# Fixed turns of the PSUM banks, and VectorE's side work set half a gap apart, in an attention and MLP kernel

## The chip, the cores and the metric

The kernel runs on one core of a Trainium2 chip. A core has five engines with a queue of instructions each: TensorE (PE in the profile, its weight loads PEld), VectorE (DVE), ScalarE (ACT), GpSimd (POOL) and SyncE (SP), which here only starts transfers. Each engine takes its own instructions strictly in the order in which the program lists them, and waits where an instruction needs the result of another engine. TensorE writes its results to PSUM, which has eight banks of 512 float32 numbers in each of 128 partitions; VectorE and ScalarE read them from there.

The metric is the device time of one execution in microseconds. Before the change the median of three executions is 1475.52 us (1472.6 to 1476.87); the profiled execution has a span of 1474.3 us.

## The reference

All data are float32. q, k and v have the shape (8, 12, 448, 64): 8 batches, 12 heads, 448 positions, 64 numbers a head. In short:

```
q_n = q / sqrt(mean(q*q) + 1e-6) * g_q          # the same for k with g_k
scores = q_n @ k_n.T / sqrt(64)                 # 448 x 448 for each batch and head
attn = exp(scores - max) / (sum + 1e-9)
x = (attn @ v), heads side by side              # 3584 rows of 12*64 = 768
h = x @ w_in                                    # 3584 x 2048
g = h - tanh(h)
out = g @ w_out                                 # 3584 x 768
```

The weights are given as float64, of which the kernel reads the two words and rounds them itself.

## The kernel before

The work is written as one long program in which the author's order is kept on every engine; the framework only adds the waits. It adds them from the tiles: an instruction that reads or writes a tile waits for the earlier ones on other engines that it must not overtake.

**Attention steps.** A step is one batch and one pair of heads, 48 in all. For a step `load` fetches q, k and v; `squares` (ScalarE) and `norm` (L365: two sums and two small operations on VectorE, two powers on GpSimd) give the factors of the norm; `norm_q` (L376) multiplies q by its factors on VectorE. `turn` (L385) transposes k and q on TensorE into two banks, and ScalarE copies them out as kT (L392) and qT (L398). `scores` (L404) multiplies them for one of four groups of keys into two banks, one for each head, and ScalarE takes the exponentials (L422). `add` (L430) adds up the exponentials of the key groups on VectorE: two additions over three full groups (L438, L439) and two over the last, half group (L442). `totals` (L470) sums them over the keys with a product with ones, and VectorE takes the reciprocal (L490). `last_values` (L444) and `values` (L457) multiply by v into two banks, and `divide` (L492) multiplies the result by the reciprocals in four operations (L498) and writes x, transposed.

**The MLP.** `mlp` is a generator of matmuls. Both layers use a form of blocked product with seven products instead of eight for each set of output blocks, in the order 1, 5, 6, 2, 3, 7, 4 (`products`, L532). In the hidden layer a product is 6 matmuls of 128x128 by 224 columns, in the output layer 8 (each shows as two records in the profile). When a product is done, its bank is read at once by one or two operations (`use`): L607 to L623 and the tanh and subtraction L589 and L590 for the hidden layer, L670 to L684 for the output layer. Products 2, 3 and 7 go on in the banks of 1, 5 and 6. A hidden layer has four sets for each batch, the output layer three. The first batch's output layer is an ordinary product instead (`project_first`, L718 and L724), because its weights are still being prepared.

**How the two are laid together.** `first_slot` works through the first steps without the MLP. From step 6 on, `slot` (L792) writes one step with four stretches of the MLP between its parts: `run(gap)` draws matmuls from the generator until as much time of TensorE is used up as the gap asks for. In a slot from step 12 on, a gap is 14 matmuls (28 records). In the order of the code: scores of key groups 0 and 1 of the next step, a gap, the transposes of the step after that, a gap, scores of the last keys, values of the last keys, sums, the other values, divisions, scores of key group 2, `add`, `norm`, a gap, `norm_q`, a gap. What stays of the MLP after the last step runs alone at the end.

**The banks.** `mm_bank` (L152) takes a bank for the MLP from a pool of three, `sc_bank` (L401) one for attention from a pool of five. In the first slots attention uses both. Each call makes a new tile of one bank, and the pool decides which of its banks that is, from what has been given back.

Of the kernel before, what the change touches and what calls it, by code (L numbers as in the profile page):

```python
# [9 lines left out]
F32 = mybir.dt.float32  # L10
# [5 lines left out]
PSUM = bass.MemoryType.PSUM  # L16
# [76 lines left out]
def bounded_path(tc, ctx, q, k, v, moe_w_in, moe_w_out, out, g_col, ident, ones, half_ones, neg_half):  # L93
# [20 lines left out]
    P = 128  # L114
# [15 lines left out]
    KF, KR = S // P, S % P  # L130
# [3 lines left out]
    def pool(name, **kw):  # L134
        return ctx.enter_context(tc.tile_pool(name=name, **kw))
# [10 lines left out]
    gp = pool("gp", bufs=1)  # L146
    wp_stack = ctx.enter_context(ExitStack())
    wp = wp_stack.enter_context(tc.tile_pool(name="wp", bufs=1))
    ps_s = pool("ps_s", bufs=5, space=PSUM)
    ps_m = pool("ps_m", bufs=3, space=PSUM)  # L150

    def mm_bank():  # L152
        return ps_m.tile([P, 512], F32, name="mm")

    loaded = {}

    def load(s, names):
        b, hp = steps[s]
        for name in names:
            src = {"q": q, "k": k, "v": v}[name]  # L160
            bufs = 3 if name == "v" else 2
            pair = src[b, 2 * hp : 2 * hp + 2]
            if name == "q":
                t = nat.tile([CP, 2, NCH, D], F32, name="q_nat", bufs=bufs)
                nc.sync.dma_start(
                    out=t.rearrange("p h c d -> p h (c d)"), in_=pair.rearrange("h (p c) d -> p h (c d)", c=NCH)
                )
            else:
                full, rest = pair[:, :K0].rearrange("h (p c) d -> h p c d", c=KF), pair[:, K0:]
                if name == "v":  # L170
                    t = nat.tile([P, 2, NCH, D], F32, name="v_nat", bufs=bufs)
                    last = t[:, :, KF]
                    nc.sync.dma_start(
                        out=t[:, :, :KF].rearrange("p h c d -> p h (c d)"), in_=full.rearrange("h p c d -> p h (c d)")
                    )
                else:
                    t = nat.tile([P, NCH, 2, D], F32, name="k_nat", bufs=bufs)
                    last = t[:, KF]
                    for h in range(2):
                        nc.sync.dma_start(out=t[:, :KF, h], in_=full[h])  # L180
                for r in range(2):
                    nc.sync.dma_start(out=last[r * KR : (r + 1) * KR], in_=rest.rearrange("h p d -> p h d"))  # L182
            loaded[name, s] = t
# [103 lines left out]
    def combine(count):  # L287
        for j, p, dst, x, y, op in combos[:count]:
            nc.vector.tensor_tensor(out=dst, in0=x, in1=y, op=op)
            if p == 7:  # L290
                kept[0] = j + 1
        del combos[:count]
# [63 lines left out]
    normed, turned, probs, sums, whole, xT, tt = {}, {}, {}, {}, {}, {}, {}  # L356
# [8 lines left out]
    def norm(s):  # L365

        sq, n = normed[s]
        rr = small.tile([P, 2, 2 * NCH], F32, name="rr", bufs=3)
        for i, rows in ((1, CP), (0, P)):
            r = rr[:rows, i]  # L370
            nc.vector.reduce_sum(r, sq[i], axis=AX.X)
            nc.vector.tensor_scalar(out=r, in0=r, scalar1=1.0 / D, scalar2=1e-6, op0=ALU.mult, op1=ALU.add)  # L372
            nc.gpsimd.tensor_tensor(out=r, in0=r, in1=neg_half[:rows], op=ALU.pow)  # L373
        normed[s] = rr, n

    def norm_q(s):  # L376
        rr, n = normed[s]
        t = loaded.pop(("q", s))
        nc.vector.tensor_tensor(
            out=n.rearrange("p c h d -> p h c d"), in0=t,  # L380
            in1=rr[:CP, 1].rearrange("p (h c) -> p h c", h=2)[:, :, :, None].to_broadcast([CP, 2, NCH, D]),
            op=ALU.mult,
        )

    def turn(s, tk, tq):  # L385

        rr, n = normed.pop(s)
        kn = loaded.pop(("k", s))
        for c in range(NCH):
            nc.tensor.transpose(tk[:, c * P : (c + 1) * P], kn[:, c].rearrange("p h d -> p (h d)"), ident)  # L390
        kT = qkp.tile([P, S], F32, name="kT")
        nc.scalar.mul(kT, tk[:, :S], g_col)  # L392
        for c in range(NCH):
            nc.tensor.transpose(  # L394
                tq[:, c * CP : (c + 1) * CP], n[:, c].rearrange("p h d -> p (h d)"), ident[:CP, :CP]
            )
        qT = qkp.tile([P, S], F32, name="qT")
        nc.scalar.copy(out=qT, in_=tq[:, :S])  # L398
        turned[s] = rr, kT, qT

    def sc_bank():  # L401
        return ps_s.tile([P, 512], F32, name="sc")

    def scores(s, c):  # L404

        rr, kT, qT = turned[s]
        halves, keys, n = (1, P, S) if c < KF else (2, KR, HS)
        name, bufs = ("p", 2) if c < 2 else ("p_full", 1) if c < KF else ("p_last", 2)
        if c == 1:
            p = probs[s, 1] = probs[s, 0]  # L410
        else:
            p = probs[s, c] = pp.tile([P, 2, 2 if c < 2 else 1, n], F32, name=name, bufs=bufs)
        tiles = [sc_bank() for _ in range(2)]
        for i in range(halves):
            for h in range(2):
                r = slice(h * D, (h + 1) * D)
                nc.tensor.matmul(  # L417
                    tiles[h][i * keys : (i + 1) * keys, :n], lhsT=kT[r, c * P : c * P + keys],
                    rhs=qT[r, i * n : (i + 1) * n], start=True, stop=True,
                )  # L420
        for h in range(2):
            nc.scalar.activation(  # L422
                p[:, h, c if c < 2 else 0, :], tiles[h][:, :n], AF.Exp, scale=rr[:, 0, 2 * c + h : 2 * c + h + 1]
            )

    def full(s):

        return probs[s, 0][:, :, 0], probs[s, 1][:, :, 1], probs[s, 2][:, :, 0]

    def add(s):  # L430

        if s <= NP + NP // 2:
            sums[s] = []
            return
        t = sp.tile([P, 2, S], F32, name="sum")
        sums[s] = [t]
        p, last = full(s), probs[s, KF][:, :, 0]
        nc.vector.tensor_tensor(out=t, in0=p[0], in1=p[1], op=ALU.add)  # L438
        nc.vector.tensor_tensor(out=t, in0=t, in1=p[2], op=ALU.add)  # L439
        for n in range(2):  # L440
            part = t[n * KR : (n + 1) * KR, :, n * HS : (n + 1) * HS]
            nc.vector.tensor_tensor(out=part, in0=part, in1=last[n * KR : (n + 1) * KR], op=ALU.add)  # L442

# [297 lines left out]
    def run(ns):  # L741

        spent[1] += ns
        while spent[0] + 1.0 < spent[1]:
            took = next(stream, None)
            if took is None:
                return
            spent[0] += took
# [10 lines left out]
    def has(s):  # L759
        return 0 <= s < NS  # L760

    def first_slot(s):

        if has(s + 1):
            scores(s + 1, 0)
            scores(s + 1, 1)
        if has(s + 2):
            turn(s + 2, mm_bank(), sc_bank())
        if s > -3:
            load(s + 4, "qk")  # L770
        squares(s + 3)
        norm(s + 3)
        if has(s):
            totals(s, mm_bank())
        if has(s + 2):
            load(s + 2, "v")
        if has(s + 1):
            scores(s + 1, KF)
        if has(s):
            av = [mm_bank() for _ in range(2)]  # L780
            last_values(s, av)
            values(s, av)
        if has(s + 1):
            scores(s + 1, 2)
            add(s + 1)
        norm_q(s + 3)
        if has(s):
            divide(s, av)
        weight(EARLY * (s + 3) // (NP + 2))
        combine(2)  # L790

    def slot(s):  # L792
        gap = gap_ns(s)
        if s < 2 * NP:
            totals(s, sc_bank())
        if has(s + 1):
            scores(s + 1, 0)
            scores(s + 1, 1)
        if has(s + 2):
            load(s + 2, "v")  # L800
        run(gap)
        if has(s + 2):
            turn(s + 2, sc_bank(), sc_bank())
        if has(s + 3):
            squares(s + 3)
        if has(s + 4):
            load(s + 4, "qk")
        run(gap)
        if has(s + 1):
            scores(s + 1, KF)  # L810
        dn = sc_bank() if s >= 2 * NP else None
        av = [sc_bank() for _ in range(2)]
        last_values(s, av)
        if s >= 2 * NP:
            totals(s, dn)
        divide(s, values(s, av))
        if has(s + 1):
            scores(s + 1, 2)
            add(s + 1)
        if has(s + 3):  # L820
            norm(s + 3)
        run(gap)
        if has(s + 3):
            norm_q(s + 3)
        run(gap)

    load(0, "qk")
    load(1, "qk")
# [335 lines left out]
```

## Time and profile before

| what | before |
|---|---|
| time, median of three | 1475.52 us |
| span of the profiled execution | 1474.3 us |
| TensorE busy | 1434.7 us (97%) |
| VectorE busy | 809.9 us (55%) |
| ScalarE busy | 455.3 us (31%) |
| GpSimd busy | 508.5 us (34%) |
| TensorE matmuls of the MLP (L553), of the chain that ended last | 63.7% |

The page's busy table tells how long each engine worked. Its ends of matmuls are modelled, so whether TensorE really had no pause is read from its waits: a wait is idle time of an engine just before an instruction, put down to the instruction on another engine that ended it. In a list in order of time, each line is a start in us, a length in us, the engine, the line of the kernel, the operation, what is written and read, how many instructions were merged into the line (x), and in brackets the idle time ahead of it with its cause. Bank tiles have the names `sc` and `mm`.

The program has four stretches: loading and the first steps (to about 109 us), the first batch of the MLP beside attention and the preparation of the weights (to about 297 us), 36 equal slots, and the last batch of the MLP alone.

### The profile page before, as it was taken

What the parts mean: (1) busy time and instruction counts of PE and PEld (TensorE: products, weight loads), DVE (VectorE), ACT (ScalarE), POOL (GpSimd) and SP (SyncE); (2) the same over time, 40 slices, a digit from 0 to 9 for tenths busy, and PEclk for the clock granted to TensorE, in tenths of its full rate; (3) what the DMA queues carried; (4) which work ended last, traced back from release to release, by engine and by line L of the source; (5) the groups of instructions that cost most, each with busy time, mean ns of one, the idle gap of its engine ahead of it and who ended that gap; (6) DMA issues with size and microseconds to landing.
All of it is one profiled execution on the core that took longest, in us unless ns stands there. A gap on an engine that the chain in (4) does not pass through costs nothing.

```text
span 1474.3 us, 26066 instructions
## 1 busy us (share of the span) xinstructions
PE 1434.7 (97%) x10272; PEld 1186.9 (81%) x10272; DVE 809.9 (55%) x1245; ACT 455.3 (31%) x850; POOL 508.5 (34%) x378
## 2 busy tenths in 40 slices
PE   6989899999999999999999999999999999999997
PEld 2558664488888888888888888888888888899997
DVE  3997888755554565347535654555555366433322
ACT  5754553133212332223322233213322233200100
POOL 4655656323331334213422233232333133312310
PEclk9999999999999999999999999999999999999999
DMA  8767787864556544654555555546555654455563
GB/s 177 171 190 201 244 252 204 230 186 148 167 145 175 174 143 144 187 166 149 185 141 169 151 163 162 163 138 182 154 167 142 167 183 135 148 166 157 187 191 97
DMA packets 268055, 250.74 MB, mean 170 GB/s; under 512 B 164884, under 2 KB 210196, under 8 KB 267924
## 3 DMA queue, kind: packets, MB, share of 16 engines
q1 hardware_dynamic: 267600, 248.97, 58.0%
q8 instruction: 84, 1.38, 0.4%
q14 instruction: 47, 0.39, 0.1%
q10 hardware_dynamic: 324, 0.00, 0.0%
HBM read 215.48 MB, written 33.42 MB: 169 GB/s over the span
## 4 chain that ended last, share of the span: by engine, by line
PE 89%; DVE 5%; DMA 2%; SPq 2%; ACT 1%; issue 1%; POOL 0%; ACTq 0%; DVEq 0%; POOLq 0%
PE mm L553 64%; PE sc L417 9%; PE sc L464 6%; PE mm L718 5%; PE sc L485 2%; PE sc L452 1%; PE sc L390 1%; PE sc L394 1%; SPq L182 1%; DVE rs L490 1%; SPq L230 1%; DVE xT L498 1%; PE mm L464 0%; DVE w_out L78 0%; DMA gT<-in_moe_w_in_dram 0%
## 5 line engine op out<-in xcount | busy, mean ns | idle before, releaser
L553 PE MATMUL mm<-xT,w_f 128*128 128x224 f32 x1392 | 280.8, 355 | 4.6 <-DVE s L619 4.6
L553 PEld LDWEIGHTS mm<-xT,w_f 128*128 128x128 f32 x1392 | 259.3, 190 | 25.5 <-issue 9.8
L553 PEld LDWEIGHTS mm<-gT,w_f 128*128 128x128 f32 x1344 | 251.4, 190 | 22.5 <-issue 11.4
L553 PE MATMUL mm<-gT,w_f 128*128 128x224 f32 x1344 | 267.7, 355 | 0.0
L373 POOL TENSOR_TENSOR rr<-rr,neg_half 112x8 f32<-112x8 f32 x96 | 157.9, 1666 | 314.3 <-DVE rr L372 314.2
L553 PE MATMUL mm<-tt,w_f 128*128 128x224 f32 x1044 | 211.2, 354 | 0.0
L553 PEld LDWEIGHTS mm<-tt,w_f 128*128 128x128 f32 x1044 | 196.1, 190 | 7.8 <-issue 7.8
L553 PE MATMUL mm<-tg,w_f 128*128 128x224 f32 x1008 | 200.4, 353 | 0.0
L553 PEld LDWEIGHTS mm<-tg,w_f 128*128 128x128 f32 x1008 | 189.5, 190 | 0.0
L417 PE MATMUL sc<-qT,kT 64*128 64x448 f32 (+1 forms) x960 | 172.9, 498 | 12.8 <-DVE xT L498 7.8
L422 ACT ACTIVATE p<-sc,rr 128x448 f32<-128x448 f32 x192 | 106.1, 637 | 200.2 <-PE sc L417 200.2
L590 POOL TENSOR_TENSOR gT<-s,th 128x448 f32<-128x448 f32 x96 | 112.8, 1182 | 153.6 <-ACT th L589 153.6
L513 POOL TENSOR_TENSOR tt<-xT,tt 128x224 f32<-128x224 f32 x23 | 32.4, 1409 | 335.5 <-DVE xT L498 335.5
L417 PEld LDWEIGHTS sc<-qT,kT 64*128 64x128 f32 (+1 forms) x960 | 62.4, 166 | 82.2 <-issue 70.1
L490 DVE RECIPROCAL rs<-sc 128x224 f32<-128x224 f32 x42 | 65.4, 1557 | 77.6 <-PE sc L485 77.5
L422 ACT ACTIVATE p_full<-sc,rr 128x448 f32<-128x448 f32 x96 | 56.0, 632 | 150.1 <-PE sc L417 150.1
L589 ACT ACTIVATE th<-s 128x448 f32<-128x448 f32 x96 | 55.4, 577 | 120.8 <-DVE s L619 63.4
L672 DVE TENSOR_TENSOR s<-mm,s 128x224 f32<-128x224 f32 x21 | 8.2, 392 | 141.8 <-PE mm L553 141.8
L464 PE MATMUL sc<-p,v_nat 128*32 128x224 f32 x1344 | 79.1, 353 | 0.0
L718 PE MATMUL mm<-gT,w_out 128*128 128x448 f32 x192 | 76.0, 552 | 0.0
L422 ACT ACTIVATE p_last<-sc,rr 128x224 f32<-128x224 f32 x96 | 37.9, 448 | 114.9 <-PE sc L417 114.9
L498 DVE TENSOR_TENSOR xT<-sc,rs 64x224 f32<-64x224 f32 x168 | 65.3, 389 | 9.7 <-PE sc L464 2.3
(118 smaller groups left out, 1623.6 us busy)
## 6 DMA issues: line engine op xcount, KB each, us to landing
w_f<-w_in SPq DMA_DIRECT2D x196, 384.0 KB, 3.4
w_f<-w_out SPq DMA_DIRECT2D x147, 512.0 KB, 3.9
w_raw<-in_moe_w_out_dram SPq DMA_DIRECT2D x16, 768.0 KB, 5.1
q_nat<-in_q_dram SPq DMA_DIRECT2D x48, 224.0 KB, 4.6
out_dram<-th SPq DMA_DIRECT2D x192, 56.0 KB, 2.2
k_nat<-in_k_dram SPq DMA_DIRECT2D x96, 96.0 KB, 3.8
v_nat<-in_v_dram SPq DMA_DIRECT2D x48, 192.0 KB, 3.8
w_in<-w_out SPq DMA_DIRECT2D x21, 384.0 KB, 6.0
```

The lines of the kernel that those rows point to most:

```text
L373: nc.gpsimd.tensor_tensor(out=r, in0=r, in1=neg_half[:rows], op=ALU.pow)
L417: nc.tensor.matmul(tiles[h][i * keys : (i + 1) * keys, :n], lhsT=kT[r, c * P : c * P + keys], rhs=qT[r, i * n : (i + 1) * n], start=True, ...
L422: nc.scalar.activation(p[:, h, c if c < 2 else 0, :], tiles[h][:, :n], AF.Exp, scale=rr[:, 0, 2 * c + h : 2 * c + h + 1])
L464: nc.tensor.matmul(av[n][r : r + BL, :HS], lhsT=v_nat[:, h, c, m * BL : (m + 1) * BL], rhs=p[c][:, h, n * HS : (n + 1) * HS], start=False, ...
L485: nc.tensor.matmul(dn[r : r + BL, :HS], lhsT=by[n], rhs=moving[2 * n + h], start=(i == 0), stop=(i == len(parts) - 1),)
L490: nc.vector.reciprocal(rs, dn[:, :HS])
L498: nc.vector.tensor_tensor(out=x[m * D : (m + 1) * D, n * HS : (n + 1) * HS], in0=av[n][m * D : (m + 1) * D, :HS], in1=rs[n * D : (n + 1) * ...
L513: eng.tensor_tensor(out=t2, in0=x22, in1=t1, op=ALU.subtract)
L553: nc.tensor.matmul(bank[:, f * HS : (f + 1) * HS], lhsT=w[:, c * width + f, :], rhs=moving[p](c), start=(first and f == 0 and c == 0), sto ...
L589: nc.scalar.activation(th, h, AF.Tanh, bias=0.0, scale=1.0)
L590: eng.tensor_tensor(out=g[:, rows, cols], in0=h, in1=th, op=ALU.subtract)
L718: nc.tensor.matmul(bank[:, :S], lhsT=w_out_row(f, n // HC)[:, n % HC * P : (n % HC + 1) * P], rhs=g[:, f, :], start=(f == 0), stop=(f == C ...
```

## The change

Two things are changed. First, the pools of PSUM banks are replaced by two tiles, one of five banks (`sc`) and one of three (`mm`), and `bank_of` hands out their banks in a fixed turn: the first, the second, and so on round. The purpose is that the order of the banks no longer depends on the pool's choice.

Second, in `slot`, the pieces of VectorE's work that nobody needs at once are moved apart. `add` is split into `add` (the two full additions) and `add_last` (the last keys). The four pieces `add`, `add_last`, `norm` and `norm_q` now each stand after half a gap of the MLP, where before `add` and `norm` stood together ahead of the third gap and `norm_q` between the third and the fourth. The purpose is that operations that empty the MLP's banks don't queue behind a run of such work. In `first_slot` the order stays as it was.

```diff
-    ps_s = pool("ps_s", bufs=5, space=PSUM)
-    ps_m = pool("ps_m", bufs=3, space=PSUM)
+    psum = {name: pool(f"ps_{name}", bufs=1, space=PSUM).tile([P, n, 512], F32, name=name) for name, n in (("sc", 5), ("mm", 3))}
+    turns = {"sc": 0, "mm": 0}
+
+    def bank_of(name):
+
+        n = turns[name] % psum[name].shape[1]
+        turns[name] += 1
+        return psum[name][:, n]
 
     def mm_bank():
-        return ps_m.tile([P, 512], F32, name="mm")
+        return bank_of("mm")
...
     def sc_bank():
-        return ps_s.tile([P, 512], F32, name="sc")
+        return bank_of("sc")
...
-        p, last = full(s), probs[s, KF][:, :, 0]
+        p = full(s)
         nc.vector.tensor_tensor(out=t, in0=p[0], in1=p[1], op=ALU.add)
         nc.vector.tensor_tensor(out=t, in0=t, in1=p[2], op=ALU.add)
-        for n in range(2):
+
+    def add_last(s):
+        last = probs[s, KF][:, :, 0]
+        for n in range(2 if sums[s] else 0):
+            t = sums[s][0]
             part = t[n * KR : (n + 1) * KR, :, n * HS : (n + 1) * HS]
             nc.vector.tensor_tensor(out=part, in0=part, in1=last[n * KR : (n + 1) * KR], op=ALU.add)
...
             add(s + 1)
+            add_last(s + 1)
...
             scores(s + 1, 2)
-            add(s + 1)
-        if has(s + 3):
-            norm(s + 3)
-        run(gap)
-        if has(s + 3):
-            norm_q(s + 3)
-        run(gap)
+        for work, n in ((add, 1), (add_last, 1), (norm, 3), (norm_q, 3)):
+            run(gap / 2)
+            if has(s + n):
+                work(s + n)
```

## The prediction

> **What bounds the kernel now.** I read first the busy table of the page, then the busy time by stretches, then the waits of TensorE from 297 to 1300 us, last the instructions in order of time inside one slot.
>
> ```profile
> PE 1434.7 (97%) x10272; PEld 1186.9 (81%) x10272; DVE 809.9 (55%) x1245; ACT 455.3 (31%) x850; POOL 508.5 (34%) x378
> ```
> ```profile
> 109.00:195.00 86.00, 80.37 (x558) 67.12 (x562) 68.34 (x95) 41.23 (x65) 47.43 (x28) 0.92 0.75 224
> ...
> 600.00:800.00 200.00, 199.34 (x1466) 170.44 (x1465) 105.24 (x165) 56.54 (x111) 64.43 (x50) 1.00 0.53 159
> ```
> ```profile
> PE mm L553 <- DVE s L619: 4.6, 6, 1.1
> ```
> The second fence has the stretch in us, then busy us of PE, PEld, DVE, ACT, POOL. From 297 us on TensorE is the bound: it is busy 199.3 of 200 us, and its only waits are six, 4.6 us together. All other engines have room. A slot lasts 28.94 us (the 48 values matmuls start at 398.37 and again at 427.31 in the chain that ended last), and 36 slots of this kind and a tail with only the MLP make up the time after 297 us. So anything that makes TensorE wait is added to the end in full.
>
> What keeps TensorE going is that a bank is emptied while it fills another:
>
> ```profile
> 1386.89 2.43 PE L553 MATMUL mm<-xT,w_f 128*128 128x224 f32 x12
> ...
> 1387.09 0.62 DVE L623 TENSOR_TENSOR s<-mm,s 128x448 f32<-128x448 f32 x1 [1.11 <-PE mm L553]
> ...
> 1389.16 4.70 PE L553 MATMUL mm<-tt,w_f 128*128 128x224 f32 x24
> 1389.36 0.53 ACT L607 COPY s<-mm 128x448 f32<-128x448 f32 x1 [0.97 <-PE mm L553]
> ```
> One product of the hidden layer is 12 records (2.27 us from start to start). Its reader starts 0.20 us after the next product has started (1389.36 - 1389.16; 1387.09 - 1386.89), beside it.
>
> [...] 0.92 granted from 109 to 195 us, where TensorE had a pause of 5.1 us.
>
> **The change, part by part.** The order of TensorE's, ScalarE's and SyncE's instructions in the built program is the same before and after; only VectorE's and GpSimd's move.
>
> Part 1, the banks. The aim is a fixed rotation. But the five "sc" banks are now one tile, and so are the three "mm" banks. I followed every wait of TensorE in the built program to the instruction that it needs. Before, a product waits for the reader of the bank it takes, three products back, and no matmul waits for a reader with nothing between, one apart. After, it waits for the **last reader of the whole tile**, whichever bank that read: the product after p=2 of the output layer waits for the copy L676 of p=2's own bank, where before it waited for L672, two products older. I counted the waits where TensorE has nothing between the matmul that is read and the matmul that waits.
>
> The price of one: the reader starts 0.20 us after the point where the next product would have started; then its duration; then the restart, which the six waits of before show:
>
> ```profile
> 493.94 0.62 DVE L619 TENSOR_TENSOR s<-mm,s 128x448 f32<-128x448 f32 x1
> ...
> 494.62 2.54 PE L553 MATMUL mm<-xT,w_f 128*128 128x224 f32 x12 [0.71 <-DVE s L619]
> ```
> The reader ends at 494.56, TensorE goes on at 494.62, and the 12 records take 2.54 in place of 2.43 us: 0.06 + 0.11 = 0.17. So one costs 0.37 us plus the reader.
>
> MLP, hidden layer, 32 sets (8 batches x 4) with the means of the groups: copy L607 0.53, add L609 0.62, L611 0.62, tanh and subtraction L589 and L590 0.54 + 0.05 + 0.62, L619 0.62, the pair L615 and L616 1.14 from start to end (494.48 to 495.62): 4.75 us a set, 152 us. L623 11 times (elsewhere attention lies between): 7. Output layer, 21 sets: L670 0.35, L672 0.39, L674 0.39, L676 0.35, the pair L678 and L679 0.65, L681 0.39: 2.52 us, 53 us; L684 four times: 2. Fixed: 333 waits x 0.37 = 123. **MLP: +337 us.**
>
> Attention, from one slot (PE starts, reader, next PE start):
>
> ```profile
> 400.13 1.61 DVE L498 TENSOR_TENSOR xT<-sc,rs 64x224 f32<-64x224 f32 x4
> ...
> 400.57 1.02 PE L417 MATMUL sc<-qT,kT 64*128 64x448 f32 x4
> ...
> 412.31 1.77 PE L417 MATMUL sc<-qT,kT 64*128 64x448 f32 x8
> ...
> 413.37 2.21 ACT L422 ACTIVATE p<-sc,rr 128x448 f32<-128x448 f32 x4 [9.68 <-PE sc L417]
> ...
> 419.86 0.55 PE L394 MATMUL sc<-ident,n 112*128 112x112 f32 x4
> 420.06 0.64 ACT L392 ACTIVATE kT<-sc,g_col 128x448 f32<-128x448 f32 x1 [2.31 <-PE sc L390]
> ...
> 426.19 0.61 PE L452 MATMUL sc<-p_last,v_nat 64*32 64x224 f32 x16
> 426.31 0.79 ACT L422 ACTIVATE p_last<-sc,rr 128x224 f32<-128x224 f32 x2 [4.14 <-PE sc L417]
> ...
> 426.73 0.59 PE L485 MATMUL sc<-sum,ones 128*32 128x224 f32 x8
> ...
> 427.46 1.56 DVE L490 RECIPROCAL rs<-sc 128x224 f32<-128x224 f32 x1 [2.82 <-PE sc L485]
> ```
> - The second pair of scores waits for both exponentials of the first: 1.06 to the first one (413.37 - 412.31), 2 x 0.57, restart 0.17, less 0.86, half of the 1.71 that the two pairs took: 1.5 us, 55 times, 83 us.
> - q's transposes wait for kT's copy: it ends at 420.70, plus 0.17, against 419.86: 1.0 us x 40 = 40 us.
> - The first value matmuls (L452) wait for both exponentials of the last keys: those ran 426.31 to 427.10, plus 0.17, against 426.19: 1.1 us x 41 = 45 us.
> - The other value matmuls (L464) wait for the reciprocal, which reads another bank: sums start 426.73, reciprocal 427.46 to 429.02, plus 0.17, against 427.31: 1.85 us x 36 = 67 us. In slots 6 to 11 the scores wait for it instead: 6 x 1.9 = 11 us.
> - The next scores wait for the four divisions, which now start only when the last value matmul is done (about 400.7): 400.7 + 1.61 + 0.2 against 400.57: 1.95 us x 41 = 80 us.
>
> **Attention: +326 us**; 24 more waits in the first slots are partly covered (0 to 1.3 us each): +20.
>
> Part 2, VectorE's side work. Two sums (1.09 + 1.23), their last part (2 x 0.80), the norm's sums (4 short ones, 1.7) and its product (1.17) no longer stand in one run behind the divisions. This can save the six waits, 4.6 us, as a burst of this work held L619 at 493.94. It adds no instruction. The norm's product still lies a slot gap ahead of the transposes that need it.
>
> Queueing: in the new order a reader that has other work ahead of it in its queue delays TensorE. Most is hidden by the 2.3 or 3.0 us of a product; not hidden are the weight pieces from 109 to 195 us (16 of about 2.75 us on VectorE, beside additions, some 1 us each), exponentials ahead of an ACT reader (some 0.7 us a slot x 36), and the slowest products of the norm (one took 4.05 us). No row shows it; I bound it by 0 and 120 us and take 40.
>
> Sum: 1475.5 + 337 + 326 + 20 - 5 + 40 = 2193, say **2190 us**. A slot would go from 28.9 to about 43 us, the tail with one batch of MLP grows by some 50 us.
>
> **The rivals.** (a) Not slower: the extra waits are met before they bind, or the banks are in effect separate. The lines where readers of 0.4 to 1.6 us follow a matmul directly speak against it, since TensorE would start in the middle of them[...]. Then the six waits and the 7.8 us on L498 before 195 us go: 1463 us. (b) Half of the waits are hidden by work that I took for serial (records still queued on TensorE, readers that start early): 1475 + 0.5 x 683 = about 1820 us. Against it: 0.20 us is the measured start of the readers on an idle engine. (c) The clock drops or queues pile up. Single pauses stay at 1 to 2 us[...]; at a mean clock of 0.9 the 1435 us of TensorE would grow by 159: about 2350 us.
>
> **How the numbers follow.** Forecast 0.86, (a) 0.03, (b) 0.04, (c) 0.07. Range: 552 exposed waits without the 0.17 restart are 94 us less, no queueing 40 less: 2060. With the whole weight load of 0.19 in place of 0.11 (44 more) and 120 of queueing (80 more): 2320. The rivals stay outside. Faster 0.02, same 0.01 (both from (a)), slower 0.97.
>
> **What would show it.** PE waits on the MLP's readers (L609, L611, L590, L616, L619, L672, L674 in the old lines) some 20 to 32 times each at 0.6 to 1.7 us; on L490, L498, L392 and L422 about 40 times each at 1 to 2 us; PE busy near two thirds, DVE, ACT and POOL busy time about unchanged; a hidden-layer product of the tail every 3.4 us or so in place of 2.27. I am wrong if TensorE's records follow each other across a product's end without a pause, or if the clock is clearly under 0.97.

## The result and the profile after

| | before | after |
|---|---|---|
| time, median of four executions | 1474.7 us (1472.6 to 1476.9) | 2241.6 us (2226.8 to 2248.3) |
| after to before | | 1.519, 95% interval 1.511 to 1.527 |
| TensorE busy | 1434.7 us (97%) | 1645.0 us (73%) |
| mean granted clock of TensorE | 0.992 | 0.940 |

The change makes the kernel slower by half. The line numbers of the kernel after are six to ten higher in the part concerned (L392, L394, L417 and L422 are now L398, L400, L423 and L428; L452, L464, L485, L490, L498 and L553 are L462, L474, L495, L500, L508 and L563; the MLP's readers move by ten). In the kernels of the experiments they can differ from these by one or two. First the busy table of the page after, and the clock of TensorE in 40 slices, in tenths:

```profile
PE 1645.0 (73%) x10272; PEld 1193.6 (53%) x10272; DVE 788.1 (35%) x1245; ACT 466.4 (21%) x850; POOL 485.9 (22%) x378
...
PEclk8889898999999998999999899899999999889999
```

The same 10272 matmuls, and about the same work on all other engines. TensorE now stands idle for 2238.9 - 1645.0 = 594 us, before 40. Its busy time also grew by 210 us. Second, whom TensorE waited for (us in total, times, longest):

```profile
PE sc L423 <- DVE xT L508: 73.3, 41, 1.9
PE sc L423 <- ACT p L428: 65.7, 48, 3.8
PE sc L474 <- DVE rs L500: 64.1, 36, 2.2
PE mm L563 <- DVE s L626: 44.1, 32, 4.2
PE mm L563 <- DVE gT L600: 42.9, 32, 1.6
PE sc L462 <- ACT p_last L428: 37.8, 41, 1.0
PE sc L400 <- ACT kT L398: 29.0, 40, 0.7
PE mm L563 <- DVE s L619: 25.2, 32, 0.8
...
PE mm L563 <- DVE s L689: 16.4, 21, 0.8
```

Read the middle number first. 32 is every set of the hidden layer, 21 every set of the output layer, 36 and 41 nearly every slot: these are not accidents of queueing but waits that are written into the program. Before, only two of these lines were there, the wait for the divisions twice (7.8 us, now L508) and the one for the first exponentials once (1.1 us, now L428). (L619 in this list is the old L609; the six waits of before on the old L619 have become 32 on L629.) The output layer in the tail, where nothing but the MLP runs, shows one wait at a time (start, length, engine, line):

```profile
2154.69 3.29 PE L563 MATMUL mm<-tg,w_f 128*128 128x224 f32 x16 [0.43 <-ACT s L680]
2158.09 0.39 DVE L682 TENSOR_TENSOR s<-mm,s 128x224 f32<-128x224 f32 x1 [5.93 <-PE mm L563]
...
2158.53 3.29 PE L563 MATMUL mm<-tg,w_f 128*128 128x224 f32 x16 [0.55 <-DVE s L682]
2161.86 0.39 DVE L684 TENSOR_TENSOR s<-mm,s 128x224 f32<-128x224 f32 x1 [3.39 <-PE mm L563]
```

Each product of 16 records starts only when the reader of the product before it has ended: L682 ends at 2158.48, TensorE goes on at 2158.53. From start to start this product takes 2158.53 - 2154.69 = 3.84 us. The same part of the kernel before:

```profile
1405.80 6.22 PE L553 MATMUL mm<-tg,w_f 128*128 128x224 f32 x32
...
1409.10 0.39 DVE L672 TENSOR_TENSOR s<-mm,s 128x224 f32<-128x224 f32 x1 [4.24 <-PE mm L553]
...
1411.86 0.35 PE L553 MATMUL mm<-gT,w_f 128*128 128x224 f32 x1
```

There the reader L672 runs beside the second of two products, and the two take 1411.86 - 1405.80 = 6.06 us, or 3.03 each.

### The profile page after: what moved, and what is told of

It reads as the page before. It is cut to its first block, busy times and chain, and to the rows that moved or that the text cites. A ratio compares the mean times of both kernels' runs of the same rounds, so it can differ in the third digit from the quotient of the medians.

```text
span 2238.9 us, 26082 instructions
## 1 busy us (share of the span) xinstructions
PE 1645.0 (73%) x10272; PEld 1193.6 (53%) x10272; DVE 788.1 (35%) x1245; ACT 466.4 (21%) x850; POOL 485.9 (22%) x378
## 4 chain that ended last, share of the span: by engine, by line
PE 70%; DVE 16%; ACT 8%; issue 4%; DMA 1%; SPq 1%; POOL 0%; DVEq 0%; ACTq 0%
PE mm L563 48%; PE sc L423 8%; PE sc L474 6%; DVE rs L500 3%; DVE xT L508 3%; PE mm L728 3%; ACT p L428 2%; ACT p_last L428 1%; PE sc L462 1%; PE sc L400 1%; ACT kT L398 1%; PE sc L495 1%; DVE gT L600 1%; DVE s L619 1%; DVE s L621 1%
## 5 line engine op out<-in xcount | busy, mean ns | idle before, releaser
L563 PE MATMUL mm<-xT,w_f 128*128 128x224 f32 x1392 | 310.6, 372 | 87.5 <-DVE gT L600 38.9
L563 PEld LDWEIGHTS mm<-xT,w_f 128*128 128x128 f32 x1392 | 261.8, 196 | 143.4 <-DVE gT L600 49.0
L563 PE MATMUL mm<-gT,w_f 128*128 128x224 f32 x1344 | 295.6, 373 | 33.9 <-DVE s L691 12.0
L423 PE MATMUL sc<-qT,kT 64*128 64x448 f32 (+1 forms) x960 | 195.0, 543 | 170.8 <-DVE xT L508 73.3
L563 PEld LDWEIGHTS mm<-gT,w_f 128*128 128x128 f32 x1344 | 256.0, 197 | 86.4 <-issue 27.1
L563 PE MATMUL mm<-tt,w_f 128*128 128x224 f32 x1044 | 226.1, 364 | 78.6 <-DVE s L626 37.5
L563 PEld LDWEIGHTS mm<-tt,w_f 128*128 128x128 f32 x1044 | 189.8, 190 | 117.1 <-DVE s L626 47.8
L563 PE MATMUL mm<-tg,w_f 128*128 128x224 f32 x1008 | 210.4, 359 | 37.5 <-DVE s L689 16.4
L563 PEld LDWEIGHTS mm<-tg,w_f 128*128 128x128 f32 x1008 | 184.4, 190 | 59.4 <-DVE s L689 23.7
L423 PEld LDWEIGHTS sc<-qT,kT 64*128 64x128 f32 (+1 forms) x960 | 57.5, 173 | 264.8 <-ACT p L428 104.1
L428 ACT ACTIVATE p<-sc,rr 128x448 f32<-128x448 f32 x192 | 111.1, 630 | 379.8 <-PE sc L423 379.8
L474 PE MATMUL sc<-p,v_nat 128*32 128x224 f32 x1344 | 104.6, 441 | 64.1 <-DVE rs L500 64.1
L428 ACT ACTIVATE p_full<-sc,rr 128x448 f32<-128x448 f32 x96 | 55.6, 630 | 400.7 <-PE sc L423 281.4
L508 DVE TENSOR_TENSOR xT<-sc,rs 64x224 f32<-64x224 f32 x168 | 65.3, 389 | 151.5 <-PE sc L474 147.9
L500 DVE RECIPROCAL rs<-sc 128x224 f32<-128x224 f32 x42 | 65.4, 1556 | 145.4 <-PE sc L495 145.3
L474 PEld LDWEIGHTS sc<-p,v_nat 128*32 128x32 f32 x1344 | 47.2, 132 | 108.7 <-DVE rs L500 79.9
L728 PE MATMUL mm<-gT,w_out 128*128 128x448 f32 x192 | 80.0, 575 | 0.0
L428 ACT ACTIVATE p_last<-sc,rr 128x224 f32<-128x224 f32 x96 | 37.6, 443 | 184.9 <-PE sc L423 184.9
```

The costliest lines, as they stand in the source:

```text
L423: nc.tensor.matmul(tiles[h][i * keys : (i + 1) * keys, :n], lhsT=kT[r, c * P : c * P + keys], rhs=qT[r, i * n : (i + 1) * n], start=True, ...
L428: nc.scalar.activation(p[:, h, c if c < 2 else 0, :], tiles[h][:, :n], AF.Exp, scale=rr[:, 0, 2 * c + h : 2 * c + h + 1])
L474: nc.tensor.matmul(av[n][r : r + BL, :HS], lhsT=v_nat[:, h, c, m * BL : (m + 1) * BL], rhs=p[c][:, h, n * HS : (n + 1) * HS], start=False, ...
L500: nc.vector.reciprocal(rs, dn[:, :HS])
L508: nc.vector.tensor_tensor(out=x[m * D : (m + 1) * D, n * HS : (n + 1) * HS], in0=av[n][m * D : (m + 1) * D, :HS], in1=rs[n * D : (n + 1) * ...
L563: nc.tensor.matmul(bank[:, f * HS : (f + 1) * HS], lhsT=w[:, c * width + f, :], rhs=moving[p](c), start=(first and f == 0 and c == 0), sto ...
```

## The experiments

Each ratio compares a kernel with the kernel before on the same chip. The experiments ran on several chips, on which the median of the kernel before was 1474.2 to 1476.9 us, so a difference of 2 or 3 us between two experiments on different chips says nothing. Diffs are against the kernel after, shortened where they have "..." or a comment.

**Eight tiles in a fixed turn.** Each bank is a tile of its own; turn and side work stay as in the change.

```diff
-    psum = {name: pool(f"ps_{name}", bufs=1, space=PSUM).tile([P, n, 512], F32, name=name) for ...}
+    psum = {name: [pool(f"ps_{name}{i}", bufs=1, space=PSUM).tile([P, 512], F32, name=f"{name}_{i}") for i in range(n)] for ...}
...
-        return psum[name][:, n]
+        return psum[name][n]
```

> The change as it is, but each of the eight banks is a tile of its own, handed out in the same fixed turn. Theory (the loss is the waits that come from five or three banks being one tile): in the built program no waits on a reader directly before are left, so the loss is gone: 1460 to 1476 us, TensorE busy 97%. Rival A (the fixed turn itself is the loss, because it takes banks that are still in use): stays above 2100. Rival B (the spread side work of VectorE is the loss): stays above 2100.

Measured: 1465.2 us, 0.992 of before (0.990 to 0.993). The same banks in the same turn, and the whole loss is gone. So it is neither the turn nor the spread side work; it is that several banks are one tile. The waits of TensorE that are left in its trace lie ahead of the equal slots; the three largest are:

```profile
PE sc L423 <- ACT p_last L428: 9.2, 4, 6.1
PE mm L396 <- DMA k_nat<-in_k_dram: 8.1, 1, 8.1
PE sc L400 <- DVE n L385: 2.9, 1, 2.9
```

**Side work spread, pools of before.**

```diff
-        return psum[name][:, n]
+        return banks[name].tile([P, 512], F32, name=name)    # banks: the two pools of before
```

> The pools of before, with the side work of VectorE spread as in the change. Theory: 1465 to 1476 us; at most the six waits of 4.6 us in total behind L619 are saved (1470.5 us). Rival B (the spread is the loss): above 2000. Rival D (the spread costs some waits of its own, as the norm's product comes later): 1476 to 1490.

Measured: 1471.6 us, 0.996 (0.995 to 0.998). Part 2 alone is a small gain of some 5 us (3 to 7 by the interval).

**Eight tiles, side work in the order of before.** As the first, with the last lines of `slot` as before.

> Eight tiles in a fixed turn, VectorE's side work in the order of before. Theory: the fixed turn takes away the waits of the scores on the divisions between 109 and 180 us (7.8 us) and nothing else: 1466 to 1476 us. Rival A (the fixed turn is the loss): above 2000.

Measured: 1469.7 us, 0.995 (0.993 to 0.996). The fixed turn by itself is a gain of some 7 us, when each bank is its own tile. In its trace the 7.8 us of waits of the scores on the divisions are gone, but those on the last exponentials grew from 3.3 to 8.0 us, so which wait the gain comes from is not shown.

**The two bank tiles, side work in the order of before.**

```diff
-        for work, n in ((add, 1), (add_last, 1), (norm, 3), (norm_q, 3)):
-            run(gap / 2)
-            if has(s + n):
-                work(s + n)
+            add(s + 1)
+            add_last(s + 1)
+        if has(s + 3):
+            norm(s + 3)
+        run(gap)
+        if has(s + 3):
+            norm_q(s + 3)
+        run(gap)
```

> The two bank tiles of the change, VectorE's side work in the order of before. Theory: the loss stays, and the first reader of the MLP after the divisions now has 5.6 us of side work ahead of it in its queue, with 2.3 to 3.0 us of matmuls beside it: about 2.9 us more a slot, 36 slots, so about 2340 us. Rival (part 2 does nothing here): 2242 us within 15.

Measured: 2307.3 us, 1.564 (1.561 to 1.566): 66 us slower than the change. So part 2 does help once TensorE waits for every reader, by two thirds of what I expected. The waits that grew are those for single readers which now have side work ahead of them; in the change the first two took 22.9 and 23.2 us:

```profile
PE mm L563 <- DVE s L629: 48.2, 32, 5.2
PE mm L563 <- DVE s L621: 44.3, 32, 4.4
```

**Only the MLP's three banks as one tile, and only attention's five.** The other banks are tiles of their own.

> The three banks of the MLP are one tile as in the change, the five of attention are five tiles; VectorE's side work spread. Theory: only the 333 waits of the MLP are left: 1465 + 337 + 20 to 40 of queueing, about 1830 us, clock near 0.99[...]. Rival (the many short pauses of the MLP are what lowers the clock from 0.99 to 0.94): clock 0.95 or less and some 1900 us.

Measured: 1836.7 us, 1.246 (1.244 to 1.248), clock 0.989.

> The five banks of attention are one tile as in the change, the three of the MLP are three tiles; side work spread. Theory: only the attention waits are left, 1465 + 326 + some 15, and the clock falls to about 0.94 as in the change, because the pauses of 1 to 2 us come close together there; that adds 50 to 100: 1850 to 1910 us. Rival (the MLP's pauses lower the clock): clock 0.99 and about 1800 us.

Measured: 1885.1 us, 1.278 (1.274 to 1.282), clock 0.939. Over the eight tiles (1465.2) the MLP's tile costs 371 us, attention's 420; together 791, against 776 for both in one kernel. The clock falls with the attention tile and not with the MLP's: in the equal slots the mean is 0.95 with the one and 1.00 with the other.

**The bank of the key sums as a tile of its own.** Attention's tile has four banks; the reciprocal no longer reads the tile that the value matmuls write.

```diff
-... for name, n in (("sc", 5), ("mm", 3))}
+... for name, n in (("sc", 4), ("dn", 1), ("mm", 3))}
...
-        dn = sc_bank() if s >= 2 * NP else None
+        dn = bank_of("dn") if s >= 2 * NP else None    # and totals(s, bank_of("dn")) in the earlier slots
```

> The change with the bank of the key sums as a tile of its own and four banks left in the attention tile: the value matmuls no longer wait for the reciprocal. Theory for the waits: 36 x 1.85 + 6 x 1.9 = 78 us less than the change, 2163 us. If the low clock comes from this pause together with the one just before it, the clock rises above 0.97 and the time falls to 2070 to 2110 us; rival: clock stays at 0.94 and the time at about 2163 us.

Measured: 2087.4 us, 1.415 (1.412 to 1.418), clock 0.979: 154 us less than the change, where 78 were forecast for the waits alone. The same with the MLP's banks as three tiles:

> MLP banks as three tiles; attention as one tile of four banks, the bank of the key sums a tile of its own. Against the kernel with all five attention banks in one tile (1885 us): if the wait of the value matmuls for the reciprocal is what lowers the clock, its 78 us go and with them some 75 us of low clock, so about 1730 us at a clock above 0.97. Rival (any of the attention waits lowers the clock about equally): clock about 0.95 and 1795 to 1810 us.

Measured: 1726.7 us, 1.169 (1.166 to 1.172), clock 0.983: 158 us less than with all five banks in one tile. Both times some 76 to 80 us more went than the forecast for the waits, and most of the clock came back. The traces split the gain: TensorE's idle time falls by 80 us in the first pair and by 91 in the second, its busy time by 71 and 67. So the part of the low clock that goes with this wait is worth some 70 us at most; at most, because a product that starts after a wait has longer records even at full clock (3.29 in place of 3.19 us for 16 records in the tail, where the clock was 1.00). The clock in 40 slices, first with the five banks in one tile, then with the sums apart:

```profile
PEclk9888878898999999998999999999999989999999
```
```profile
PEclk9899989999999999999999999999999999999999
```

A digit 9 stands for anything from 0.90, so these rows show best the stretch ahead of the equal slots. There the mean clock is 0.88 and 0.95, and the longest pauses are of 10.2 and 8.1 us, so that stretch does not show which pauses it goes with. But in the equal slots, with no pause over 2.2 us in either kernel, it is 0.95 and 0.99. In those slots busy time falls by 54 us in the first pair and by 53 in the second.

**The spread only from step 12 on.** The traces of the four kernels at 1465 to 1477 us allow a split: the start of the last pair of ordinary products of the first output layer (before the equal slots; L718, which is L726 and L728 in the others), and the start of the tail. In the chains that ended last of, in turn, the kernel before, the spread alone, the eight tiles in the old order, the eight tiles with the spread:

```profile
282.77 12.22 PE mm L718 x32
...
1328.59 137.93 PE mm L553 x728
```
```profile
286.50 12.22 PE mm L726 x32
...
1324.70 137.92 PE mm L561 x728
```
```profile
276.86 12.22 PE mm L728 x32
...
1322.28 137.92 PE mm L563 x728
```
```profile
282.12 12.22 PE mm L728 x32
...
1320.33 137.92 PE mm L563 x728
```

Between the two lines lie 1045.8, 1038.2, 1045.4 and 1038.2 us: the spread is worth 7.6 us in the equal slots with the pools and 7.2 with the eight tiles. Ahead of them it seemed to lose 4 to 5 us. So I left it out there (eight tiles; in steps 6 to 11 the order of before, from step 12 on the spread), beside the eight tiles once more.

> Eight tiles in a fixed turn; VectorE's side work spread only in the slots from step 12 on, and in the order of before in steps 6 to 11. The traces of the four kernels without extra waits say that the spread wins some 7 us in the 36 equal slots and loses 4 to 5 us before them. Theory: the loss can be taken out alone: about 1460 us, below the eight tiles with the spread everywhere (1465.2). Rival (the loss ahead of the equal slots is made up later or comes from elsewhere): 1465 within 2.

> The eight tiles with the spread everywhere once more, on the same chip for the comparison with the spread from step 12 on: 1463 to 1468 us.

Measured: 1460.4 us, 0.990 (0.989 to 0.992), against 1462.9 us, 0.993 (0.991 to 0.994), for the eight tiles with the spread everywhere. This is the fastest kernel of the study, 1% below the kernel before. But the reason I gave is weak: in this second trace the eight tiles with the spread everywhere reach the same point at 276.87 us, where the first reached it at 282.12, and the new kernel at 275.45. The early part of one kernel differs by 5 us between two executions; in the slower of the two, TensorE's clock was also at half for 24 us ahead of the equal slots, in the other for 14. Some 2 us of gain is what the medians show, with intervals that just touch.

## Why the prediction was right

The direction, the mechanism of the waits and the range were right; 2190 us was forecast, 52 us too low. Step by step:

- **The mechanism.** A tile of several banks makes TensorE wait for the last reader of any of them. Shown by the eight tiles: the same turn and order without the shared tile, 1465 us. In their trace TensorE waits 0.3 us in all for the MLP's readers, so the waits between different banks came from the program alone.
- **The number of waits.** I had counted 32 for the readers of the hidden layer, 21 for the output layer, 36 to 41 for attention. The profile has just these, if 13 waits that it shows without a cause belong to two readers of the MLP that fall 6 and 7 short (L617 with 26 of 32, L684 with 14 of 21); the exponentials' 55 show as 48 behind L428 of the first groups, 6 behind that of the last full group, and one behind neither.
- **The price of one, 0.37 us plus the reader.** In the tail: 3.84 - 3.03 = 0.81 for a reader of 0.39, so 0.42. Close. An equal slot took 44.8 us, where about 43 were forecast.
- **MLP: +337, with some of the 40 for queueing.** Measured with the MLP's tile alone: +371 us, with 333 waits, the number that was counted.
- **Attention: +326 and +20.** With the sums apart 78 of it goes, leaving 268; measured +262 us (1726.7 - 1465.2).
- **Part 2: -5.** Measured alone 5.3 us by the medians (1476.9 - 1471.6), and 7.6 us in the equal slots, so it also saves more there than the six waits.
- **The clock: nothing.** This step failed. The forecast rests on my estimate that pauses of 1 to 2 us are too short to lower the clock, which no trace had shown; a lower clock was left to rival (c). In the equal slots the pauses were as short as forecast, 2.2 us at most, and the clock still fell to 0.95 there. (Ahead of them six waits of the scores for the reciprocal took 21.3 us, the longest 6.2, where 11 were forecast.) The two pairs with and without the wait for the reciprocal put the price at 71 and 67 us of busy time at most.
- **The missing 48 us.** Attention's tile cost 420 us in place of 346, 74 more. This is the clock in the main: against the eight tiles, TensorE's idle time grew by 309 us, which is no more than the forecast, and its busy time by 106. Against it stand the MLP with its queueing (371 for up to 377), the 15 us by which the two tiles overlap, and the 5 us by which the eight tiles are faster than the start that was forecast: 74 - 6 - 15 - 5 = 48, which leads from 2193 to 2241 us. That these smaller terms took off a third of the error is luck; the range, which reached to 2320 us, would have held without them.
- **Rival (a)** named 1463 us for a kernel in which the banks are in effect separate: the eight tiles gave 1465.2 and 1462.9.

I had written that I would be wrong if the clock was clearly under 0.97. It was, and only the size of the error stayed small, since some 70 us are 9% of a loss of 767.

What stays open: whether the wait for the reciprocal alone would lower the clock as much, since every kernel that had it also had the wait of 0.9 us just ahead of it (the kernels with the sums apart had that shorter wait alone, at a clock of 0.99 in the equal slots), and how the time ahead of the equal slots splits between single executions.

## What to carry to other kernels

Where a framework derives waits from tiles, the tile and not the bank is the unit of waiting: buffers that are to be filled while others are emptied must be tiles of their own, even if one tile with an index does the same on paper (1465 against 2242 us here). A change of buffers can be judged before any run by following each wait of the busiest engine to the instruction that it needs, and counting those with nothing of that engine's own work between. And when all engines wait in turn, side work ahead of a reader in its queue costs many times what it did: the spreading of it was worth 5 us in the pipelined kernel and 66 us in the serial one.

## What the runs showed of the hardware

In the equal slots of the change, where no pause was over 2.2 us, TensorE's clock was at half in 28 stretches. One case from the trace after, in order of time:

```profile
1950.07 0.61 PE L462 MATMUL sc<-p_last,v_nat 64*32 64x224 f32 x16 [0.90 <-ACT p_last L428]
...
1950.61 0.58 PE L495 MATMUL sc<-sum,ones 128*32 128x224 f32 x8
...
1953.02 1.72 PE L474 MATMUL sc<-p,v_nat 128*32 128x224 f32 x16 [1.83 <-DVE rs L500]
```

TensorE waits 0.90 us, works 1.1 us, waits 1.83 us; then 16 records take 1.72 us where they took 0.94 before:

```profile
398.19 0.94 PE L464 MATMUL sc<-p,v_nat 128*32 128x224 f32 x16
```

All 48 value matmuls lasted 4.75 us in the chain that ended last, in place of 2.27 before. The granted clock by stretches (it is the third number from the end) shows how long this lasts:

```profile
1940.00:1953.00 13.00, 8.48 (x68) 6.11 (x66) 2.34 (x3) 1.95 (x4) 0.00 (x0) 0.96 0.29 81
1953.00:1964.00 11.00, 9.21 (x59) 5.17 (x60) 3.92 (x6) 1.16 (x2) 3.34 (x4) 0.50 0.01 1
1964.00:1997.00 33.00, 26.02 (x146) 20.51 (x145) 6.63 (x11) 3.79 (x8) 0.00 (x0) 0.97 0.46 126
1997.00:2008.00 11.00, 8.96 (x59) 4.88 (x60) 3.96 (x7) 1.16 (x2) 3.34 (x4) 0.50 0.00 0
```

Some 11 us or a little more at half speed follow the pause in this slot and in the next. It isn't so in each slot: the mean over the equal slots, about 430 to 2041 us, is 0.95. The 28 stretches at half speed in the trace's record of the clock are 167 us together. Of these, 18 begin at the wait for the reciprocal and 9 at the wait for the divisions, which comes 4.2 to 6.5 us later. With the sums apart (MLP and attention tiles kept) 12 are left, 44 us together, all at the wait for the divisions. The MLP's 333 pauses, nearly all of 0.4 to 1.5 us with 2 to 3 us of matmuls between, left the mean clock at 0.989, and at 1.00 in the equal slots. So the sum of the pauses does not explain the clock: the MLP's tile cost 371 us at 0.989, attention's 420 at 0.939, of which 309 were idle time. In attention the pauses come close together with little work between, as 0.90 and 1.83 us around 1.1 us of work above. Whether it is the nearness, the length or the kind of work between that counts was not tested apart.
